# The first stage of an induced-attention and maxout kernel as one table of operations, with one group cut into a narrow and four shorter chunks

## The chip, the core and the metric

The kernel runs on one core of one Trainium2 chip. The metric is the device time of one execution in microseconds. The core has five engines that run their own instruction streams in order and wait for each other through semaphores: TensorE (PE, with PEld for its weight loads), VectorE (DVE), ScalarE (ACT), GpSimd (POOL), and SyncE (SP), which here issues nearly all DMA transfers.

## What is computed

The reference attends twice and then applies a maxout layer. Shapes: x is 4 x 12544 x 128, inducing is 32 x 128, w1, w2 and w3 are 128 x 768, w_out is 768 x 128.

```python
def mab(q, kv):
    s = scale * (q @ kv.transpose(0, 2, 1))
    s = s - s.max(-1, keepdims=True)
    a = np.exp(s)
    a /= a.sum(-1, keepdims=True) + 1e-09
    return a @ kv
h = mab(I, x)
return mab(x, h).astype(np.float32)
...
h = np.maximum(np.maximum(x @ w1, x @ w2), x @ w3)
return (h @ w_out).astype(np.float32)
```

In the first attention 32 inducing rows look at all 12544 tokens of a batch and give h, 32 x 128. In the second each token looks at the 32 rows of h. Its result goes through the maxout of three products and then through w_out.

## The kernel before

**Tiling.** A batch has 98 tiles of 128 tokens. They lie in seven groups: group 0 is short (2 tiles), groups 1 to 6 have 16 tiles each. Phase 1 is the first attention and works by group; it ends in hT, the transposed h divided by its sums. Phase 2 works by chunk: the short group is one chunk of 256 columns, and a full group gives four chunks of 512 columns. So a batch has 25 chunks and the kernel 100. Each chunk is six slots, one for each 128 of the 768 hidden columns.

**Algebra.** Since an output row of the second attention is probabilities times h, h is multiplied into the weights ahead of time (`first_products` for batch 0, `combine_products` later): wcat holds w1 - w2 and w3 - w2 in pairs and, in its last 128 columns, w2 times w_out (`prep_products`, kept by `keep_products`). The products of h with wcat are kept as a high and a low part in us. A slot is then: a matmul pu (L669), a relu by ACT (L684), a matmul pv (L675), a maximum by DVE (L702), a rounded copy hi by ACT (L691), the remainder lo by POOL (L699) or, for the slots listed in LOWVEC, by DVE (L705), and three matmuls into the accumulator (L727, L728, L729), six slots later (LAG). The first slot of a chunk adds one matmul with the last columns of us (L726).

**Weights.** They arrive as 64-bit numbers. `convert` makes 32-bit ones in steps: t, T, p, r and d on DVE, z on ACT, A (an addition) on POOL or, as a, on DVE, and S (subtraction of w2) on POOL. The digit in front is the matrix: 0 is w2, 1 is w_out, 2 is w1, 3 is w3. WORK lists which steps stand in which round of phase 1.

**Phase 1 of batch 0** is written out in `phase1_first`. For a group: load, 16 PE transposes (L272) with ACT copies (L274), products with the inducing rows (`attend_products`), maximum (`attend_max`), a column of it (`attend_column`), its spread over partitions by a matmul (`attend_spread`), the least value (`attend_least`), exponentials (`attend_weights`), a transpose (`attend_transpose`), sums on PE (`attend_sums`) and their copy (`attend_keep`). Then the groups are joined with weights (`combine_least` to `combine_states`). LOADS sets the order of the first transfers: short group, group 1 in four pieces, group 2, w2, group 3, w_out, groups 4 and 5, w1, group 6, w3. There are five buffers for full groups (XB).

**Filling.** Behind hT, the string ORDER interleaves the softmax of groups 0 (a) and 1 (b), the first products, dummy matmuls (`keep_busy`, d) and the first slots (s), until `main` runs the rest by a plan of slots. Phase 1 of batch b + 1 runs within phase 2 of batch b. `probs` brings the probabilities of a chunk into place: by PE transposes for the short group, by four DMAs on SP for the others.

All five engines keep the order in which the program writes their instructions (`manual_schedule`).

Of the kernel before, what the change touches and what calls it, by code (L numbers as in the profile page):

```python
# [8 lines left out]
F32 = mybir.dt.float32  # L9
# [16 lines left out]
def kernel(ctx, tc, x, xt, ind_t, w1, w2, w3, w_out, out):  # L26
    nc = tc.nc
# [23 lines left out]


    ORDER = "a a a a b a a b 0 c d m b a b a b a p d b 1 c s b b b s S m b q 2 c s 3 c s d s s d s"
# [70 lines left out]
    raws = []  # L124
    def first_loads():
        for what in LOADS:
            if what < NG:
                xg_next[(0, what)] = load_group(0, what, pieces=4 if what == 1 else 1)
            else:
                raws.append(load_raw(srcs[what - NG]))  # L130
# [79 lines left out]
    w2t = []  # L210

    def transpose_w2():
        for h in range(2):
            tpw = bank_v[h]
            for k in range(3):
                j = 3 * h + k
                nc.tensor.transpose(out=tpw[:, k * P : (k + 1) * P], in_=wf[:, 0, j * P : (j + 1) * P], identity=ident)
            w2h = hp.tile([P, 512], F32, name="w2h", tag="ru", bufs=3)
            nc.scalar.copy(out=w2h[:, : 3 * P], in_=tpw[:, : 3 * P])
            w2t.extend(w2h[:, k * P : (k + 1) * P] for k in range(3))  # L220

    def prep_products():

        wo = wf[:, 1, :].rearrange("p (j c) -> p j c", c=C)
        pw = bank_u[1]
        for j in range(NJ):
            nc.tensor.matmul(out=pw[:, :C], lhsT=w2t[j], rhs=wo[:, j, :], start=(j == 0), stop=(j == NJ - 1))

    def keep_products():
        nc.scalar.copy(out=wcat[:, 2 * DF :], in_=bank_u[1][:, :C])  # L230

    def prep_out():
        wo = wf[:, 1, :].rearrange("p (j c) -> p j c", c=C)
        nc.scalar.copy(out=wo_hi, in_=wo)
        nc.gpsimd.tensor_sub(out=wo_lo, in0=wo, in1=wo_hi.bitcast(F32))

# [3 lines left out]
    def start_batch(b):  # L240
        st = state[b] = {"xT": {}, "xg": {}, "a": {}, "s": {}}
# [25 lines left out]
    def transpose_x(b, gi, k):  # L267
        st = state[b]
        n = min(4, groups[gi]["nt"] - k)
        tps = (bank_u + bank_v)[k // 4]  # L270
        for i in range(n):
            nc.tensor.transpose(out=tps[:, i * P : (i + 1) * P], in_=st["xg"][gi][:, k + i, :], identity=ident)  # L272
        xv4 = st["xT"][gi].rearrange("p (q t l) -> p t q l", q=NQ, l=M)
        nc.scalar.copy(out=xv4[:, k : k + n, :, :], in_=tps[:, : n * P].rearrange("p (t q l) -> p t q l", q=NQ, l=M))  # L274
# [12 lines left out]
    def attend_max(b, gi):  # L287
# [5 lines left out]
        st["mq"] = mq  # L293

    def attend_column(b):
# [3 lines left out]
        nc.scalar.mul(out=md, in_=quad, mul=st["mq"])  # L299
        st["md"] = md  # L300

    def attend_spread(b, bank=None):
# [3 lines left out]
        nc.tensor.matmul(out=st["mp"][:, :NQ], lhsT=sel, rhs=st["md"], start=True, stop=True)  # L306
# [91 lines left out]
    def phase1_first():  # L398

        start_batch(0)  # L400
        nc.sync.dma_start(out=iT, in_=ind_t)
        nc.scalar.mul(out=iT, in_=iT, mul=scale)
        first_loads()
        def half(gi, k):
            if gi < NG:
                if k == 0:
                    start_group(0, gi)
                for i in (k, k + 4):
                    transpose_x(0, gi, i)

        start_group(0, 0)
        keep_busy(6, bank_o[1])
        transpose_x(0, 0, 0)
        keep_busy(2, bank_o[1])
        attend_products(0, 0, bank_a[0])
        attend_max(0, 0)
        attend_column(0)
        half(1, 0)
        attend_spread(0, bank_o[0])
        attend_least(0, 0)  # L420
        half(1, 8)
        work(WORK[0])
        st = state[0]
        for gi in range(NG - 1):
            last = gi == NG - 2
            attend_products(0, gi + 1, bank_a[(gi + 1) % 2])
            attend_weights(0, gi)
            half(gi + 2, 0)
            attend_max(0, gi + 1)
            attend_column(0)  # L430
            half(gi + 2, 8)
            if gi > 0:
                attend_sums(0, gi - 1, bank_o[1])
                attend_keep(0, gi - 1)
            attend_transpose(0, gi)
            if not last:
                work(WORK[gi + 1][0])
            attend_spread(0, bank_o[0])
            attend_least(0, gi + 1)
            if gi == 3:  # L440
                transpose_w2()
            if last:
                prep_products()
            else:
                work(WORK[gi + 1][1])
        combine_least(st)
        work(WORK[NG - 1])
        combine_weights(st)
        attend_weights(0, NG - 1)
        keep_products()  # L450
        attend_sums(0, NG - 2, bank_o[1])
# [536 lines left out]
```

## Time and profile before

| | us |
|---|---|
| median of three runs | 822.78 (822.32 to 823.0) |
| span of the profiled execution | 821.3 |
| hT written (end of L514) | 42.41 |
| first matmul of a 512-column chunk (L669) | 54.39 |
| first accumulation of group 2 of batch 0 (L726) | 93.99 |

The profile is of one execution. Its span runs from the first to the last instruction; the time of a run includes what lies around it. "L272" is line 272. In rows of an engine's order of time the first number is the start, the second the time covered, and brackets give the idle time in front and who ended it. Rows of groups give the count, the total busy time and the mean of one in ns.

### The profile page before, as it was taken

To read this page: it belongs to the slowest core of one execution; us is meant where nothing else is said; L and a number is where in the kernel's file an instruction comes from. 1 tells how busy PE (TensorE), PEld (TensorE's weight loads), DVE (VectorE), ACT (ScalarE), POOL (GpSimd) and SP (SyncE) were. 2 spreads that over 40 slices of the span, in tenths; PEclk is the share of its full clock that TensorE was granted. 3 is DMA by queue.
4 is the path that set the end of the run, shared out by engine and by line. 5 is a ranking of instruction groups with operands and counts; after the bars stand their busy time and mean duration, and the time that the engine had idled before them with its cause. 6 is when DMAs were issued, how large, how long until landed. Compare 5 with 4: busy or idle time off the path is not lost.

```text
span 821.3 us, 14725 instructions
## 1 busy us (share of the span) xinstructions
PE 809.0 (98%) x4604; PEld 634.0 (77%) x4604; DVE 627.4 (76%) x1090; ACT 743.5 (91%) x1558; POOL 650.1 (79%) x521
## 2 busy tenths in 40 slices
PE   7989999999999999999999999999999999999998
PEld 5757778778788787777778777877778788787886
DVE  4977778777787687787786877877778788778864
ACT  5779889898899898898999988989889899899996
POOL 1269779778799697787888977977879889888887
PEclk9999999999999999999999999999999999999999
DMA  8844534433443544344334352431223222222221
GB/s 325 310 137 151 188 88 161 161 120 107 136 139 121 154 154 162 84 162 159 110 106 142 116 205 83 159 119 58 63 80 89 71 78 77 65 81 76 63 78 52
DMA packets 44206, 102.51 MB, mean 125 GB/s; under 512 B 9568, under 2 KB 13536, under 8 KB 38880
## 3 DMA queue, kind: packets, MB, share of 16 engines
q1 hardware_dynamic: 43984, 101.44, 38.5%
q8 instruction: 37, 0.61, 0.3%
q14 instruction: 41, 0.34, 0.1%
q10 hardware_dynamic: 144, 0.13, 0.0%
HBM read 48.12 MB, written 25.69 MB: 90 GB/s over the span
## 4 chain that ended last, share of the span: by engine, by line
PE 95%; DMA 2%; DVE 1%; SPq 1%; ACT 1%; issue 0%; ACTq 0%; DVEq 0%
PE acc L727 17%; PE pv L675 16%; PE acc L728 16%; PE acc L729 16%; PE pu L669 16%; PE aux L585 3%; PE acc L726 3%; PE acc L346 3%; PE aux L282 2%; DMA xg<-in_x_dram 2%; PE acc L306 0%; PE pu L272 0%; SPq L100 0%; PE pv L272 0%; PE aux L551 0%; DMA pT<-pl 0%
## 5 line engine op out<-in xcount | busy, mean ns | idle before, releaser
L699 POOL TENSOR_TENSOR lo<-h,hi 128x512 fp32r<-128x512 f32 (+1 forms) x502 | 634.9, 1295 | 129.8 <-ACT hi L691 84.0
L702 DVE TENSOR_TENSOR h<-pv,ru 128x512 f32<-128x512 f32 (+1 forms) x600 | 404.2, 675 | 167.8 <-PE pv L675 81.2
L684 ACT ACTIVATE ru<-pu 128x512 f32<-128x512 f32 (+1 forms) x600 | 375.3, 626 | 52.6 <-PE pu L669 49.7
L691 ACT CAST hi<-h 128x512 fp32r<-128x512 f32 (+1 forms) x600 | 386.4, 644 | 0.4 <-DVE h L702 0.3
L727 PE MATMUL acc<-hi,wo_hi 128*128 128x512 f32 (+1 forms) x600 | 236.9, 395 | 0.0
L675 PE MATMUL pv<-pT,us 128*128 128x512 f32 (+1 forms) x600 | 232.1, 387 | 0.3 <-DVE h L702 0.3
L669 PE MATMUL pu<-pT,us 128*128 128x512 f32 (+1 forms) x600 | 231.5, 386 | 0.4 <-DMA pT<-pl 0.4
L728 PE MATMUL acc<-hi,wo_lo 128*128 128x512 f32 (+1 forms) x600 | 231.5, 386 | 0.0
L729 PE MATMUL acc<-lo,wo_hi 128*128 128x512 f32 (+1 forms) x600 | 231.2, 385 | 0.0
L727 PEld LDWEIGHTS acc<-hi,wo_hi 128*128 128x128 f32 x600 | 112.7, 188 | 30.0 <-issue 8.7
L675 PEld LDWEIGHTS pv<-pT,us 128*128 128x128 f32 x600 | 112.6, 188 | 24.2 <-DVE h L702 1.6
L669 PEld LDWEIGHTS pu<-pT,us 128*128 128x128 f32 x600 | 112.6, 188 | 23.9 <-DMA pT<-pl 0.6
L729 PEld LDWEIGHTS acc<-lo,wo_hi 128*128 128x128 f32 x600 | 112.7, 188 | 23.0
L728 PEld LDWEIGHTS acc<-hi,wo_lo 128*128 128x128 f32 x600 | 112.8, 188 | 21.1
L705 DVE TENSOR_TENSOR lo<-h,hi 128x512 fp32r<-128x512 f32 x98 | 71.3, 727 | 0.7 <-ACT hi L691 0.7
L744 ACT COPY o<-acc 128x512 f32<-128x512 f32 (+1 forms) x99 | 61.1, 617 | 0.0
L726 PE MATMUL acc<-pT,us 128*128 128x512 f32 (+1 forms) x100 | 38.7, 387 | 0.0
L346 PEld LDWEIGHTS acc<-xg,aT 128*32 128x32 f32 x768 | 21.1, 110 | 11.4 <-issue 6.8
L282 PE MATMUL aux<-xT,iT 128*32 128x512 f32 x192 | 25.3, 598 | 1.6 <-ACT xT L274 1.6
L346 PE MATMUL acc<-xg,aT 128*32 128x128 f32 x768 | 25.6, 274 | 0.0
L585 PE MATMUL aux<-xT,hT 128*32 128x512 f32 x192 | 25.1, 603 | 0.0
L192 POOL TENSOR_TENSOR rest<-rest,t 128x768 f32<-128x768 f32 x3 | 5.5, 1824 | 24.3 <-DVE rest L184 24.3
(119 smaller groups left out, 445.4 us busy)
## 6 DMA issues: line engine op xcount, KB each, us to landing
out_dram<-o SPq DMA_DIRECT2D x95, 256.0 KB, 2.0
xg<-in_x_dram SPq DMA_DIRECT2D x23, 1024.0 KB, 6.9
xT<-in_xt_dram SPq DMA_DIRECT2D x18, 1024.0 KB, 5.2
pT<-ph SPq DMA_DIRECT2D x192, 64.0 KB, 2.0
pT<-pl SPq DMA_DIRECT2D x192, 64.0 KB, 2.0
raw<-in_w_dram SPq DMA_DIRECT2D x3, 768.0 KB, 9.5
us<-uh SPq DMA_DIRECT2D x24, 52.0 KB, 1.9
us<-ul SPq DMA_DIRECT2D x24, 52.0 KB, 1.9
```

Of the source, the lines that this page charges most:

```text
L346: nc.tensor.matmul(out=hps[q * M : (q + 1) * M, :C], lhsT=aT[:, t * M : (t + 1) * M], rhs=xg[:, t, :], start=(t < NQ), stop=(t + NQ >= nt),)
L669: nc.tensor.matmul(out=pu[:, :w], lhsT=state[c.b]["us"][:, 2 * j * P : (2 * j + 1) * P], rhs=c.pT[:, :w], start=True, stop=True)
L675: nc.tensor.matmul(out=pv[:, : d.w], lhsT=state[d.b]["us"][:, (2 * j + 1) * P : (2 * j + 2) * P], rhs=d.pT[:, : d.w], start=True, stop=True,)
L684: nc.scalar.activation(out=ru[:, :w], in_=pu[:, :w], func=AF.Relu)
L691: nc.scalar.copy(out=hi[:, : c.w], in_=h[:, : c.w])
L699: nc.gpsimd.tensor_sub(**args)
L702: nc.vector.tensor_max(out=h[:, : d.w], in0=pv[:, : d.w], in1=relus.pop(s)[:, : d.w])
L705: nc.vector.tensor_sub(**low)
L726: nc.tensor.matmul(out=c.acc[:, :w], lhsT=us[:, 2 * DF :], rhs=c.pT[:, :w], start=True, stop=False)
L727: nc.tensor.matmul(out=c.acc[:, :w], lhsT=wo_hi[:, j, :], rhs=c.hh[j][:, :w], start=False, stop=False)
L728: nc.tensor.matmul(out=c.acc[:, :w], lhsT=wo_lo[:, j, :], rhs=c.hh[j][:, :w], start=False, stop=False)
L729: nc.tensor.matmul(out=c.acc[:, :w], lhsT=wo_hi[:, j, :], rhs=c.hl[j][:, :w], start=False, stop=(j == NJ - 1))
```

## The change

Batch 0's phase 1 and the filling behind it become one string of operations, FIRST, that is walked through once; each engine gets its part in that order. Capital letters are the steps of a group (T transposes, C their copies, P products, M maximum, D column, R spread, N least, E exponentials, X transpose, S sums, K their copy); digit and letter are the weight steps as before; c, l, i and hT join the groups; qS, qA and qB are the score products of the short group, the first four tiles of group 1 and its other twelve; s, a and b are the steps of their softmaxes; U, h, l, g and H are the first products, their high parts, low parts on DVE, copies and low parts on POOL; s with a digit is a slot and z a step of the second stage.

- The short group is last in phase 1 (TURN), and the loads are: group 1 in two pieces, groups 2 and 3, w2, group 4, w1, group 5, w3, group 6, the short group, w_out. The inducing rows are loaded from ACT's queue. XB is 6.
- Of w_out's work, d, the rounded copy, the remainder, and the product with w2 stand behind hT, as does half of w2's transposes. The addition for w3 is POOL's. The dummy matmuls are nine at the start and none behind hT.
- Group 1 of batch 0 is five chunks: one of 4 tiles over all quadrants (512 columns, probabilities by PE transposes, as for the short group) and four of 384 columns. Batch 0 has 26 chunks, the kernel 101. The lists LOWHEAD and LOWREST say which of their remainders DVE makes.
- The second stage starts four slots behind the first, not six, until slot 16.
- The score products of group 2 of batch 0 move from ORDER to the plan of the main loop.

```diff
-    XB = 5
+    XB = 6
-    LOADS = (0, 1, 2, 7, 3, 8, 4, 5, 9, 6, 10)
-    WORK = (
-        "",
-        ("0t 0T 0p 0z", "0r 0A"),
-        ("1t 1T 1p 1z", "1r 1A"),
-        ("0d 1d", "2t"),
-        ("2T 2p 2z", "2r 2A"),
-        ("3t 3T 3z", "3p 2d 2S"),
-        "3r",
-        "3a 3d 3S",
-    )
+    LOADS = (1, 2, 3, 7, 4, 9, 5, 10, 6, 0, 8)
+    TURN = (1, 2, 3, 4, 5, 6, 0)
+    HEAD = 4
+    LOWHEAD = (1, 4)
+    LOWREST = (0, 17, 19, 21, 23)
+    FIRST = (
+        "B9 B4 T11 T10 T12 C10 C11 T13 C12 C13 P1 T20 C20 M1 T21 D1 T22 T23 R1 N1 C21 C22 C23 E1 T30 T31 T32 "
+        "P2 C30 X1 T33 C32 0t C31 C33 M2 0T S1 D2 R2 P3 T42 0p N2 0r 0z T43 M3 K1 E2 D3 C43 X2 0A T40 R3 S2 "
+        "2t N3 T41 C40 C42 2T T50 2p T53 E3 0d T52 C41 C50 C53 X3 T51 C52 C51 2r P4 2A 2z M4 3t P5 M5 K2 D4 "
+        "R4 N4 T62 T61 T60 T63 3z D5 E4 3T 2d C61 C60 C63 3p R5 S3 C62 X4 N5 1t 2S T00 P6 3r K3 E5 C00 1z M6 "
+        "S4 P0 X5 M0 D6 K4 R6 N6 D0 E6 W1 1T R0 S5 n2 N0 X6 3A cl E0 1p K5 S6 cw X0 lw 1r cm 3d lt iv K6 S0 "
+        "1A cg123456 K0 w1 cg0 hT W0 qS 1d qA 3S aT sT qB w0 am Oh sm ax ae sx bT se U1 sr U0 ar si h1 ai sp "
+        "g1 ap su sh au bm sl U2 ah bx js h0 h2 ks al l0 Ol Gp H1 be g2 Gk s0 br bi bp ja ka s1 bu U3 H2 n3 "
+        "s2 4h s3 4l bt s4 bh s5 bl y2 z0 s6 y3 z1 s7 z2 s8 z3 z4 s9 s10 z5 s11 z6 s12 z7 "
     )
-    ORDER = "a a a a b a a b 0 c d m b a b a b a p d b 1 c s b b b s S m b q 2 c s 3 c s d s s d s"
...
-    def prep_out():
+    def prep_high():
+        nc.scalar.copy(out=wo_hi, in_=wf[:, 1, :].rearrange("p (j c) -> p j c", c=C))
+
+    def prep_low():
         wo = wf[:, 1, :].rearrange("p (j c) -> p j c", c=C)
-        nc.scalar.copy(out=wo_hi, in_=wo)
         nc.gpsimd.tensor_sub(out=wo_lo, in0=wo, in1=wo_hi.bitcast(F32))
...
-        nc.sync.dma_start(out=iT, in_=ind_t)
+        nc.scalar.dma_start(out=iT, in_=ind_t)
...
-    def scores_products(b, gi, bank):
+    def scores_products(b, gi, bank, first=0, last=None):
...
+                out=bank[q * M : (q + 1) * M, :n],
+                lhsT=st["hT"][:, :M],
+                rhs=xT[:, q * w + first * M : q * w + last * M],
...
     class Chunk:
-        def __init__(self, n, b, gi, q):
-            self.n, self.b, self.gi, self.q = n, b, gi, q
-            self.w = GT * M if q is not None else groups[gi]["nt"] * P
+        def __init__(self, n, b, gi, q, first=0, last=None):
+            self.n, self.b, self.gi, self.q, self.first = n, b, gi, q, first
+            self.last = last or groups[gi]["nt"]
+            self.w = (self.last - first) * (P if q is None else M)
...
-            if self.q is None or (self.gi == 1 and self.q == k == 0):
-                return False
+            if self.q is None:
+                return self.last == HEAD and k in LOWHEAD
+            if self.first == HEAD:
+                return NJ * self.q + k in LOWREST
...
+            parts_ = [(None, 0, None)]
+            if groups[gi]["nt"] == GT:
+                parts_ = [(q, 0, None) for q in range(NQ)]
+                if b == 0 and gi == 1:
+                    parts_ = [(None, 0, HEAD)] + [(q, HEAD, None) for q in range(NQ)]
...
-                elif b > 0 or g > 1:
+                else:
                     first.append((scores_products, b, g + 1, bank_a[0]))
...
-            if s >= LAG:
-                c, j = slots[s - LAG]
-                stage2(c, j)
-                if j == NJ - 1:
-                    over = c
+            if done[0] <= s - (LAG if s >= begins[0] + 4 else LAG - 2):
+                over = second()
```

More of the change, by code (lines that the diff above doesn't have):

```diff
@@ L265, in load_channels, with transpose_x, keep_x @@
         state[b]["xg"][gi] = xg_next.pop((b, gi))
[L267 to L274, printed above, removed]
+    def transpose_x(gi, i):
+        st = state[0]
+        if gi not in st["xT"]:
+            start_group(0, gi)
+        tps = (bank_u + bank_v)[i]
+        for k in range(min(4, groups[gi]["nt"])):
+            nc.tensor.transpose(out=tps[:, k * P : (k + 1) * P], in_=st["xg"][gi][:, 4 * i + k, :], identity=ident)
+    def keep_x(gi, i):
+        n = min(4, groups[gi]["nt"])
+        tps = (bank_u + bank_v)[i]
+        xv4 = state[0]["xT"][gi].rearrange("p (q t l) -> p t q l", q=NQ, l=M)
+        nc.scalar.copy(
+            out=xv4[:, 4 * i : 4 * i + n, :, :], in_=tps[:, : n * P].rearrange("p (t q l) -> p t q l", q=NQ, l=M)
+        )
     def attend_products(b, gi, bank):
@@ L529, in first_products @@
         st["up"][which] = up, st["us"][:, cs]
+    half = slice(2 * M, P)
     def first_high(st, which):
@@ L731, in finish @@
     def finish(c):
-        at = groups[c.gi]["at"] + (c.q or 0) * c.w
+        g = groups[c.gi]
+        at = g["at"] + (c.q or 0) * g["nt"] * M + c.first * M
         o = op.tile([P, 512], F32, name="o", tag="o", bufs=3)
+        if c.q is None and c.last < g["nt"]:
+            nc.scalar.copy(
+                out=o.rearrange("p (q t l) -> p t q l", q=NQ, l=M), in_=c.acc.rearrange("p (t q l) -> p t q l", q=NQ, l=M)
+            )
+            nc.sync.dma_start(
+                out=out[c.b, :, at : at + g["nt"] * P].rearrange("p (q n) -> p q n", q=NQ)[:, :, : c.w // NQ],
+                in_=o.rearrange("p (q n) -> p q n", q=NQ),
+            )
+            return
         if c.n == len(chunks) - 1:
@@ L756 @@
         for gi in range(NG):
-            full = groups[gi]["nt"] == GT
-            for q in range(NQ) if full else [None]:
-                chunks.append(Chunk(len(chunks), b, gi, q))
-    nch = len(chunks) // B
+            parts_ = [(None, 0, None)]
[3 more added lines that the diff above has]
+                    parts_ = [(None, 0, HEAD)] + [(q, HEAD, None) for q in range(NQ)]
+            for part in parts_:
+                chunks.append(Chunk(len(chunks), b, gi, *part))
     LAG = 6
@@ L765 @@
     plan = [[] for _ in range(len(slots) + LAG)]
-    per_batch = nch * NJ
-    short = NJ if groups[0]["nt"] < GT else 0
+    begins = [min(c.n for c in chunks if c.b == b and c.q is not None) * NJ for b in range(B)]
     WIN = NQ * NJ
@@ L801 @@
     for b in range(B):
-        base = b * per_batch + short
+        base = begins[b]
         n = b + 1
@@ L870, with second, main @@
             burst(s0 + 15, *second)
-    def main():
-        over = None
-        for s in range(len(slots) + LAG + 1):
+    done = [0]
+    def second():
+        c, j = slots[done[0]]
+        done[0] += 1
+        stage2(c, j)
+        return c if j == NJ - 1 else None
+    def main(start, over):
+        for s in range(start, len(slots) + LAG + 1):
             if s >= LAG:
@@ new lines @@
+        for step in FIRST.split():
+            kind, rest = step[0], step[1:]
+            if step in names:
+                names[step]()
+            elif kind in steps and not rest.isdigit():
+                next(steps[kind])
+            elif kind == "c":
+                combine_groups(st, [int(g) for g in rest[1:]], bank_u[0])
+            elif kind.isdigit():
+                convert(int(kind), rest)
+            elif kind == "s":
+                advance()
+            elif kind == "z":
+                if over:
+                    finish(over)
+                over = second()
+            elif kind == "f":
+                finish(over)
+                over = None
+            elif kind == "y":
+                probs(tails[rest])
+            else:
+                one[kind](*[int(v) for v in rest])
@@ L934 @@
+        for gen in steps.values():
+            assert next(gen, None) is None
+        main(pipe["next"], over)
 _GT = 16
```

304 lines of the change are left out of this document (139 added, 165 removed).

## The prediction

> **What bounds the kernel now.** I began with the page's busy shares. Then I cut the span into stages, and inside the first of them I read each engine's instructions in order of time.
>
> ```profile
> span 821.3 us, 14725 instructions
> PE 809.0 (98%) x4604; PEld 634.0 (77%) x4604; DVE 627.4 (76%) x1090; ACT 743.5 (91%) x1558; POOL 650.1 (79%) x521
> 10.00:20.00 10.00, 8.06 (x64) 4.67 (x64) 6.79 (x11) 7.89 (x18) 2.32 (x2) 1.00 1.03 410
> 13.54:42.41 28.87, 25.68 (x347) 18.50 (x346) 26.05 (x45) 21.34 (x52) 9.64 (x7) 1.00 0.85 319
> 42.41:54.39 11.98, 10.14 (x62) 5.50 (x62) 9.67 (x24) 8.03 (x21) 6.46 (x7) 1.00 0.37 114
> 54.39:60.92 6.53, 6.53 (x43) 5.37 (x44) 4.80 (x9) 5.94 (x13) 5.32 (x6) 1.00 0.64 185
> 60.92:93.99 33.07, 33.07 (x190) 25.25 (x188) 25.36 (x45) 30.37 (x67) 27.43 (x23) 1.00 0.53 173
> 93.99:800.00 706.01, 706.01 (x3822) 557.17 (x3821) 548.44 (x945) 657.30 (x1368) 585.25 (x465) 1.00 0.36 113
> ```
>
> The columns of the stages are length, then busy time of PE, PEld, DVE, ACT and POOL, granted clock, DMA share and GB/s. From 60.92 us on PE has no gap. What the change does after group 1 of batch 0 therefore costs or brings nothing, unless it alters PE's own work; PE's 706.01 of 706.01 us is the cover. The time is decided by when PE gets there. My marker is the first accumulation of group 2 of batch 0 (L726, at 93.99 below): after it both kernels have the same PE work left. So the forecast is where that marker lands.
>
> ```profile
> 55.31 0.28 PE L726 MATMUL acc<-pT,us 128*128 128x256 f32 x1
> 55.42 0.27 PE L727 MATMUL acc<-hi,wo_hi 128*128 128x256 f32 x1
> 93.99 0.39 PE L726 MATMUL acc<-pT,us 128*128 128x512 f32 x1
> 94.21 0.39 PE L727 MATMUL acc<-hi,wo_hi 128*128 128x512 f32 x1
> ```
>
> Durations overlap; the pitch of starts is what a matmul costs: 0.22 to 0.23 us with 512 columns (I use 0.2265), 0.11 to 0.12 with 256 (0.115). This is almost proportional, so 384 columns should pitch at 0.171. Before the marker lie two stages, split by h (the tile hT, which ends at 42.41).
>
> **Part 1, up to h: VectorE's list.** DVE is busy 26.05 of the 28.87 us between its first weight step and hT.
>
> ```profile
> 0.75 0.39 SPq L401 DMA_DIRECT2D iT<-in_ind_t_dram  x1
> 1.19 0.42 SPq L100 DMA_DIRECT2D xgs<-in_x_dram  x1
> 13.54 0.56 DVE L171 TENSOR_SCALAR t<-raw 128x768 uint32<-128x768 uint32 x1 [0.97 <-DMA raw<-in_w_dram]
> 14.14 0.96 DVE L175 SCALAR_TENSOR_TENSOR t<-raw,t 128x768 uint32<-128x768 uint32 x1
> 15.13 0.56 DVE L180 TENSOR_SCALAR pw<-t 128x768 uint32<-128x768 uint32 x1
> 15.61 0.15 DVE L312 TENSOR_REDUCE mneg<-acc 128x1 f32<-128x4 f32 x1
> 15.72 0.96 DVE L184 SCALAR_TENSOR_TENSOR rest<-raw,pw 128x768 f32<-128x768 uint32 x1
> 16.60 0.68 DVE L292 TENSOR_REDUCE mq<-aux 128x1 f32<-128x512 f32 x1
> 17.20 0.70 DVE L336 STREAM_TRANSPOSE aT<-a 128x512 f32<-128x512 f32 x1
> ...
> 37.37 0.38 DVE L477 TENSOR_TENSOR sw<-sel,w 128x224 f32<-128x224 f32 x1
> ...
> 38.53 0.95 DVE L192 TENSOR_TENSOR rest<-rest,t 128x768 f32<-128x768 f32 x1
> 39.51 0.96 DVE L196 SCALAR_TENSOR_TENSOR dst<-size,rest 128x768 f32<-128x768 f32 x1
> 41.66 0.35 DVE L509 RECIPROCAL rec<-rec 128x32 f32<-128x32 f32 x1
> 42.12 0.29 DVE L514 TENSOR_TENSOR hT<-pu,rec 128x128 f32<-128x128 f32 x1
> ```
>
> Where the list starts: w2's raw weights land at 13.54 (DVE waited 0.97 us for them). The new load order puts groups 1, 2 and 3 ahead of w2 and takes the short group out, so 0.9 MB more stands in front: 2.2 us at 410 GB/s. The first big load leaves SP where iT now leaves, 0.9 us sooner than in before, since iT moves to ACT's queue and the short group back; its pieces are also larger. I credit 1.0 us (bounds 0 and 1.5). So w2 lands at about 14.7, between 14.2 and 15.7.
>
> What is in the list: after this point the table has for DVE four of t, T, p, r (by the starts above 0.60, 0.98, 0.50, 0.90: 11.9), three d (0.95 each: 2.85), the maxima and transposes of groups 2 to 6 (0.60 and 0.62 each: 6.1) and of group 0 (an estimate of 0.4), six least-values (0.9), and the joining steps up to hT (the rows of sw, rec and hT, 1.0, and four of about 0.1 each: 1.45). Sum 23.6. The addition of row 38.53 (0.95) goes to POOL. The d of w_out moves behind hT. Both leave the list.
>
> What it waits for: once for group 2's products, which now stand behind three transposes of group 3 on PE (0.25), and small hand-overs, for which I take 0.8 of the 2.8 us that DVE idles in this stage now (bounds 0 and 2.8). And one thing that the new order creates:
>
> ```profile
> L196 DVE SCALAR_TENSOR_TENSOR wf<-size,rest x2: 945/1298/1652, 22.8 to 24.4; 128x768 f32<-128x768 f32 x2
> 21.81 1.83 POOL L192 TENSOR_TENSOR rest<-rest,t 128x768 f32<-128x768 f32 x1 [2.66 <-DVE rest L184]
> ```
>
> A d that starts while POOL is in an addition takes 1.65 us, not 0.95: it ends about 0.8 us after POOL's end at 23.64. In the table the steps "1r cm 3d" run directly after each other, and POOL begins w_out's addition when 1r ends. So 3d waits for most of its 1.83 us; hT needs the group sums on PE anyway, so I take 1.15 us of this (bounds 0 and 1.4). Sum: 14.7 + 23.6 + 0.25 + 0.8 + 1.15 = 40.5, say **hT at 40.6, 1.8 us sooner**. PE and ACT do not set it: each loses w_out's work here, and their busy times (25.68 and 21.34) stand under DVE's.
>
> **Part 2, from h to the marker.**
>
> ```profile
> 42.85 0.27 DVE L598 STREAM_TRANSPOSE aux<-aux 128x64 f32<-128x64 f32 x1 [0.44 <-PE aux L585]
> 50.42 1.22 SPq L654 DMA_DIRECT2D pT<-ph  x2
> 54.39 0.50 PE L669 MATMUL pu<-pT,us 128*128 128x512 f32 x1 [0.38 <-DMA pT<-pl]
> 54.98 0.60 ACT L684 ACTIVATE ru<-pu 128x512 f32<-128x512 f32 x1 [0.84 <-PE pu L669]
> 55.48 0.40 ACT L691 CAST hi<-h 128x256 fp32r<-128x256 f32 x1
> 55.77 0.61 ACT L684 ACTIVATE ru<-pu 128x512 f32<-128x512 f32 x1
> 56.26 0.41 ACT L691 CAST hi<-h 128x256 fp32r<-128x256 f32 x1
> L217 PE MATMUL pv<-ident,wf 128*128 128x128 f32 x6 | 0.9, 282 | 0.0
> L227 PE MATMUL pu<-wf,w2h 128*128 128x128 f32 x12 | 1.6, 282 | 0.0
> L219 ACT COPY w2h<-pv 128x384 f32<-128x384 f32 x2 | 0.9, 537 | 0.0
> L234 ACT CAST wo_hi<-wf 128x768 fp32r<-128x768 f32 x1 | 0.8, 835 | 0.0
> L396 PE MATMUL pu<-ident 128*128 128x128 f32 x16 | 2.6, 287 | 0.6 <-ACT pT L651 0.5
> ```
>
> Now hT to the marker takes 51.58 us. PE's work in it is 10.14 less 2.6 of dummy matmuls (L396), then, for the six short slots after 54.39, twelve 512-column and eighteen 256-column matmuls and a few others (5.25 of 6.53), then 33.07: 45.8. Slack is 5.8.
>
> Moved in: half of w2's transposes (0.45), the six products with w_out (1.6), four transposes for the 4-tile chunk (0.75, by the mean of the 128-column rows). The six extra slots bring 31 matmuls but no columns: at pitches 0.2265 and 0.171 that is 0.1. Together 2.9. The dummies go; they cost nothing, as they stood in slack.
>
> The slack that stays: the table puts w_out's d first behind hT on DVE, and POOL's subtraction 3S, released by 3d, is then running, so by the row above it ends some 1.75 us after hT, at 42.35. Behind it on DVE wait both score transposes, which now start at 42.85; this gains only 0.5 us there. From there ACT is the dense engine: w_out's cast 0.8, exponentials and probability copies 2.0, six evictions of first products at 0.5, w2's product 0.2, twelve evictions of the short chunk at 0.29 (the pitch of the 256-column rows; 512 pitch at 0.49) less one, 3.3: 9.3, with hand-overs 9.8. So the 4-tile chunk's first relu comes at about 52.2, against 54.98, without the DMA wait in row 54.39, as its probabilities come from PE transposes. Between hT (40.6) and there PE has 10.0 us of work in 11.6: slack 1.6. Over the next six slots ACT again asks 0.8 to 1.0 a slot, and I leave 0.8. Together 2.4, against 5.8. Behind the 4-tile chunk the 384-column chunks get their probabilities by DMA, issued when the larger softmax ends, about 52.3; in before it took 4 us from issue (row 50.42) to use (row 54.39), and the head's six slots cover some 6.
>
> Sum: 45.8 + 2.9 + 2.4 = 51.1 after hT: the marker at 91.7 against 93.99. **The span falls by 2.3 to 819.0.** The runs' median 822.78 stands 1.5 above the profiled span, and I keep that: **820.5**.
>
> One rule speaks against taking the dummies out. The granted clock is 1.00 in every stage above, also with PE busy 8.06 of 10 us. The Trainium skill, "TensorE: Matmul & The Clock Gate", in its part on the HAM clock gate, says that the clock halves after an idle window of some 3.4 us. The trace has no gap so long with which to test it.
>
> **Rivals.**
> - *The hand-overs stay* (chance 0.22). DVE waits its 2.8 us and the lock in full; hT comes at 42.6 or later, and only the shorter filling gains. Against before: 0 to 1, so about 822.3. For it: the same chain of maximum, column, spread and least runs once per group in both. Against it: the table puts a weight step between its parts.
> - *ACT becomes the bound; slower* (0.12). ACT's busy time from hT to the marker is 8.03 + 5.94 + 30.37 = 44.3 of 51.6. Added: the cast, one copy of w2 and the product (1.5), the evictions (at an interpolated 0.39 for 384 columns, 48 of them and 12 of 512 against 48 of 512: 1.1), copies for the split softmax (1.0): 47.9. If the 7.3 us that it now idles stay, the marker is at 40.6 + 55.2 = 95.8 and the time 824.6. It decides from 5.5 us of idle on. Against it: ACT's idle is mostly waiting in the filling, which the table is dense in.
> - *The filling is tighter* (0.10): no lock on 3d and 1d, w2 at 14.2, hT at 39.2 and 50.3 to 51.1 behind it; the marker at 89.5 to 90.3, so 818.3 to 819.1. With no hand-overs either it is 817.5.
> - *The clock drops behind hT* (0.02), where the dummies stood: at half pace PE's 10.0 us there take 20 in place of 11.6, so about 829.
>
> **How the numbers follow.** The forecast has 0.54, with a range of its own of 819 to 821.8 from w2's landing and the hand-overs. A measurement of this kernel can tell about 0.2% (1.65 us) from no change: faster is below 821.1, slower above 824.4. Faster: 0.46 of the forecast, the tighter filling's 0.10 and 0.01 of the first rival, 0.57. Slower: most of the ACT case and the clock, 0.12. Same: 0.31. The range from 816.8 to 823.8 leaves out most of the ACT case, the clock and the end of the tighter filling, under 0.2.
>
> **What would show it.** Right: w2's first step on DVE near 14.7; hT ending between 39.5 and 41.5; 3d and the d behind hT over 1.3 us long; the first 512-column relu near 52; no dummies and under 3 us of PE gaps behind hT; the marker near 91.7; the same 706 us behind it. Wrong: a marker shift other than the shift of the span, which would mean that the change works in the later part; a PE that waits for ACT or POOL in the 384-column chunks; a granted clock under 1.00; hT no sooner than 42.

## The result and the profile after

The changed kernel takes 827.84 us (median of 5, 826.8 to 828.18) against 822.78 (822.32 to 823.0): a ratio of 1.0057, with a 95% interval of 1.0042 to 1.0072. It is slower by 5.06 us, outside the range of the prediction, and on the side that was given a chance of 0.12. The description of the change has one slip: the table begins with thirteen dummy matmuls ("B9 B4"), not nine.

Of the page after, the first line; then a cut into the stages that the prediction used (hT ends at 42.31, the short chunk's first accumulation starts at 53.80, that of the 4-tile chunk at 59.46, the marker is at 96.37). Columns as before: length, busy time of PE, PEld, DVE, ACT, POOL, granted clock, DMA share, GB/s.

```profile
span 825.8 us, 15091 instructions
```

```profile
13.54:42.31 28.77, 24.54 (x342) 16.90 (x339) 27.19 (x45) 20.87 (x52) 10.36 (x7) 1.00 0.52 197
42.31:53.80 11.49, 8.65 (x61) 5.41 (x61) 11.15 (x30) 8.12 (x23) 6.34 (x6) 1.00 0.79 327
53.80:59.46 5.66, 5.54 (x32) 4.58 (x32) 4.60 (x9) 5.36 (x14) 4.75 (x6) 1.00 0.19 47
59.46:96.37 36.91, 36.87 (x241) 30.39 (x239) 29.38 (x59) 33.03 (x83) 27.13 (x26) 1.00 0.56 180
96.37:800.00 703.63, 702.43 (x3803) 553.56 (x3802) 550.51 (x944) 653.06 (x1361) 579.10 (x458) 1.00 0.36 113
```

```profile
96.37 0.40 PE L694 MATMUL acc<-pT,us 128*128 128x512 f32 x1
```

The marker moved from 93.99 to 96.37, by +2.38; the span grew by 4.5. So about half of the loss arises ahead of the marker and half behind it, where PE, busy 706.01 of 706.01 us before, now has 1.2 us of gaps in 703.63. Before hT, DVE is busy 27.19 of 28.77 us (26.05 of 28.87 before), although steps were taken off it.

**Ahead of hT.** The changed kernel's DVE in order of time, rows of weight steps, and POOL's rows beside the long ones:

```profile
15.36 0.52 DVE L171 TENSOR_SCALAR t<-raw 128x768 uint32<-128x768 uint32 x1
...
25.77 1.79 DVE L171 TENSOR_SCALAR t<-raw 128x768 uint32<-128x768 uint32 x1
...
31.04 1.51 DVE L171 TENSOR_SCALAR t<-raw 128x768 uint32<-128x768 uint32 x1
...
38.86 2.56 DVE L196 SCALAR_TENSOR_TENSOR dst<-size,rest 128x768 f32<-128x768 f32 x1
...
42.02 0.29 DVE L462 TENSOR_TENSOR hT<-pu,rec 128x128 f32<-128x128 f32 x1
42.46 1.74 DVE L196 SCALAR_TENSOR_TENSOR wf<-size,rest 128x768 f32<-128x768 f32 x1
```

```profile
25.33 1.82 POOL L192 TENSOR_TENSOR rest<-rest,t 128x768 f32<-128x768 f32 x1 [4.49 <-DVE rest L184]
30.05 2.07 POOL L200 TENSOR_TENSOR wcat<-dst,wf 128x768 f32<-128x768 f32 x1 [2.90 <-DVE dst L196]
...
38.72 1.89 POOL L192 TENSOR_TENSOR rest<-rest,t 128x768 f32<-128x768 f32 x1 [3.35 <-DVE rest L184]
...
41.57 1.81 POOL L200 TENSOR_TENSOR wcat<-dst,wf 128x768 f32<-128x768 f32 x1 [0.70 <-DVE rec L456]
```

Read the two together. Every stretched row overlaps a POOL row and ends 0.4 us (t) to 0.8 us (d) after it: the t at 25.77 ends at 27.56, POOL's addition at 27.15. So do a t at 20.08 (1.19) and a T at 34.90 (1.28), not shown. The t that overlaps none takes 0.52. The same line in the kernel before (ns: least, median, most) shows no such stretch; its longest, 694, is the one that overlaps the end of a POOL addition:

```profile
L171 DVE TENSOR_SCALAR t<-raw x4: 560/578/694, 13.5 to 31.5; 128x768 uint32<-128x768 uint32 x4
```

The Trainium skill, "SBUF — State Buffer", section "Who interferes with whom", has tensor_scalar in its two-port modes, and operations with two inputs in SBUF, use ports that DVE shares with GpSimd; whoever comes first holds them for a whole instruction, and the other blocks. The rows agree: 1.79 against 0.52 us. Below this is called the lock.

**Behind the marker.** PE's first accumulations of the short chunk of batch 1 and of the chunk behind it, before and after, then DVE's and POOL's rows after:

```profile
250.07 0.28 PE L726 MATMUL acc<-pT,us 128*128 128x256 f32 x1
256.55 0.40 PE L726 MATMUL acc<-pT,us 128*128 128x512 f32 x1
```

```profile
252.46 0.28 PE L694 MATMUL acc<-pT,us 128*128 128x256 f32 x1
258.39 0.51 PE L640 MATMUL pv<-pT,us 128*128 128x512 f32 x1 [0.47 <-DVE h L667]
259.94 0.40 PE L694 MATMUL acc<-pT,us 128*128 128x512 f32 x1
```

```profile
256.14 1.59 DVE L670 TENSOR_TENSOR lo<-h,hi 128x512 fp32r<-128x512 f32 x1 [0.94 <-PE acc L697]
257.66 0.68 DVE L667 TENSOR_TENSOR h<-pv,ru 128x512 f32<-128x512 f32 x1
```

```profile
255.89 1.29 POOL L664 TENSOR_TENSOR lo<-h,hi 128x512 fp32r<-128x512 f32 x1 [1.75 <-ACT hi L656]
```

The distance is 6.48 us before and 7.48 after. DVE makes a remainder (L670) that waits 0.94 for PE to free its buffer and takes 1.59, and the next maximum stands behind it. The median of this line is 0.68; here POOL's own remainder, from 255.89 to 257.18, lies in its way, so the lock seems to have a part in this too. Behind the short chunk of batch 2 the distance grows alike, from 6.47 to 7.48 us; behind that of batch 3 it is 7.23 in both kernels. The diff ahead of the prediction shows why: the old condition `self.q is None or (self.gi == 1 and self.q == k == 0)` kept the first slot of group 1 of every batch off DVE; its second half went. The list of changes doesn't name it, and the prediction gives it no price.

### The profile page after: what moved, and what is told of

It reads as the page before. It is cut to its first block, busy times and chain, and to the rows that moved or that the text cites. A ratio compares the mean times of both kernels' runs of the same rounds, so it can differ in the third digit from the quotient of the medians.

```text
span 825.8 us, 15091 instructions
## 1 busy us (share of the span) xinstructions
PE 811.1 (98%) x4641; PEld 638.7 (77%) x4641; DVE 638.6 (77%) x1110; ACT 744.8 (90%) x1574; POOL 648.1 (78%) x521
## 4 chain that ended last, share of the span: by engine, by line
PE 95%; DVE 3%; ACT 1%; issue 0%; POOL 0%; ACTq 0%; DVEq 0%; POOLq 0%
PE acc L695 17%; PE pv L640 16%; PE acc L696 16%; PE acc L697 16%; PE pu L634 16%; PE aux L538 3%; PE acc L694 3%; PE aux L289 2%; PE acc L355 2%; PE pu L405 1%; PE pu L273 1%; PE acc L315 0%; PE pv L273 0%; DVE h L667 0%; DVE wf L196 0%
## 5 line engine op out<-in xcount | busy, mean ns | idle before, releaser
L664 POOL TENSOR_TENSOR lo<-h,hi 128x512 fp32r<-128x512 f32 (+2 forms) x501 | 631.0, 1290 | 137.2 <-ACT hi L656 94.1
L667 DVE TENSOR_TENSOR h<-pv,ru 128x512 f32<-128x512 f32 (+2 forms) x606 | 405.1, 670 | 159.6 <-PE pv L640 99.0
L649 ACT ACTIVATE ru<-pu 128x512 f32<-128x512 f32 (+2 forms) x606 | 375.2, 619 | 53.5 <-PE pu L634 50.4
L656 ACT CAST hi<-h 128x512 fp32r<-128x512 f32 (+2 forms) x606 | 386.9, 638 | 1.8 <-DVE h L667 1.5
L695 PE MATMUL acc<-hi,wo_hi 128*128 128x512 f32 (+2 forms) x606 | 238.0, 393 | 0.0
L640 PE MATMUL pv<-pT,us 128*128 128x512 f32 (+2 forms) x606 | 233.9, 386 | 1.8 <-DVE h L667 1.4
L634 PE MATMUL pu<-pT,us 128*128 128x512 f32 (+2 forms) x606 | 233.3, 385 | 0.2 <-ACT ru L649 0.2
L696 PE MATMUL acc<-hi,wo_lo 128*128 128x512 f32 (+2 forms) x606 | 232.7, 384 | 0.0
L697 PE MATMUL acc<-lo,wo_hi 128*128 128x512 f32 (+2 forms) x606 | 232.5, 384 | 0.0
L670 DVE TENSOR_TENSOR lo<-h,hi 128x512 fp32r<-128x512 f32 (+1 forms) x105 | 77.8, 741 | 4.2 <-PE acc L697 2.7
```

The lines of the kernel that those rows point to most:

```text
L634: nc.tensor.matmul(out=pu[:, :w], lhsT=state[c.b]["us"][:, 2 * j * P : (2 * j + 1) * P], rhs=c.pT[:, :w], start=True, stop=True)
L640: nc.tensor.matmul(out=pv[:, : d.w], lhsT=state[d.b]["us"][:, (2 * j + 1) * P : (2 * j + 2) * P], rhs=d.pT[:, : d.w], start=True, stop=True,)
L649: nc.scalar.activation(out=ru[:, :w], in_=pu[:, :w], func=AF.Relu)
L656: nc.scalar.copy(out=hi[:, : c.w], in_=h[:, : c.w])
L664: nc.gpsimd.tensor_sub(**args)
L667: nc.vector.tensor_max(out=h[:, : d.w], in0=pv[:, : d.w], in1=relus.pop(s)[:, : d.w])
```

## The experiments

Theory A: two faults, the dropped exclusion (behind the marker) and POOL in the way of DVE (ahead of hT), hide a table that works as forecast. Rivals: the small additions of the softmax, the second stage's early start, the clock, the split. Runs are compared by medians; the number of executions and the range stand in brackets. The kernel before, run beside them, had medians of 822.59 to 822.86.

**The first slot.** e1_slot0 puts the exclusion back into the changed kernel; e2_before_slot0 takes it out of the kernel before.

```diff
+            if self.gi == 1 and self.q == k == 0:
+                return False
             return NJ * self.q + k in (LOWVEC if self.b + 1 < B else LOWLAST)
```

> The changed kernel, with one condition of before put back: the remainder of slot 0 of group 1 in batches 1 to 3 is POOL's again and not DVE's. The marker (first accumulation of group 2 of batch 0) stays at 96.4 us. Theory A (DVE is late at that slot behind the short chunk of batches 1 and 2, 1.0 us each, the two steps by which the kernels drift apart from +2.4 to +4.4 us): the drift after the marker goes, the time falls by 2.0 us to about 825.8. Rival (more load buffers or the third softmax buffer shift something there): the drift stays, the time stays within 0.5 us of 827.8.

825.79 us (11, 824.64 to 826.24), ratio 1.0028 (1.0017 to 1.0039): 2.05 less, as theory A asked. The marker is hardly moved (96.25), and the distance is 6.48 again:

```profile
252.35 0.28 PE L696 MATMUL acc<-pT,us 128*128 128x256 f32 x1
...
258.83 0.40 PE L696 MATMUL acc<-pT,us 128*128 128x512 f32 x1
```

> The kernel before, with that condition taken out: slot 0 of group 1 is DVE's in all four batches. Theory A: PE waits for DVE behind the short chunks of batches 1 and 2, 1.0 us each, and perhaps in batch 0: 2 to 3 us more than 822.8, so 824.8 to 825.8. Rival: within 0.5 us of 822.8.

826.55 us (8, 826.01 to 829.46), ratio 1.0042 (1.0025 to 1.0059): the old kernel loses 3.9, more than expected. Here the edit acts in batch 0 too, where the changed kernel has lists of its own (LOWHEAD, LOWREST); in its profiled execution (828.29) the distance behind batch 0's short chunk is 7.64 us (55.00 to 62.63), in the kernel before 5.61 (55.31 to 60.92). So the surplus shows there.

**POOL beside DVE.** e4_poolshort leaves POOL's two conversion steps all their instructions and waits, but only 16 of 768 columns for A and 4 of each 128 for S, so most of w1 - w2, w3 - w2 and the corrections is not computed; wcat is filled with zeros first.

```diff
-            (nc.gpsimd if step == "A" else nc.vector).tensor_add(out=c["rest"], in0=c["rest"], in1=c["t"].bitcast(F32))
+            nc.gpsimd.tensor_add(out=c["rest"][:, :16], in0=c["rest"][:, :16], in1=c["t"].bitcast(F32)[:, :16])
```

> The changed kernel, with POOL's weight additions and subtractions in phase 1 cut to a few columns (wcat is set to zero at the start; the conversion is left incomplete). Theory B: DVE's steps beside them fall to their lengths alone (t from 1.19, 1.79 and 1.51 to 0.56 us; 3d from 2.56 to 0.95; the d of w_out from 1.74 to 0.95), hT comes 3.5 to 5.5 us sooner, near 37 to 39 in place of 42.3, and the time falls by 3 to 5 us. Rival C (the load order or the chain through PE and ACT sets hT): DVE's steps shorten, but hT stays within 1.5 us of 42.3 and DVE waits instead.

823.88 us (12, 822.97 to 824.52), ratio 1.001 (1.0 to 1.0019): 3.96 less than the changed kernel. hT ends at 39.70, not at the 37 to 39 that theory B asked. DVE's rows in order of time:

```profile
16.81 0.52 DVE L172 TENSOR_SCALAR t<-raw 128x768 uint32<-128x768 uint32 x1
...
37.46 0.97 DVE L197 SCALAR_TENSOR_TENSOR dst<-size,rest 128x768 f32<-128x768 f32 x1
...
39.41 0.29 DVE L463 TENSOR_TENSOR hT<-pu,rec 128x128 f32<-128x128 f32 x1 [0.49 <-PE pu L437]
39.62 0.95 DVE L197 SCALAR_TENSOR_TENSOR wf<-size,rest 128x768 f32<-128x768 f32 x1
```

From the first t to the end of hT it is 22.89 us, against 26.95: the lock costs 4.06 there, and 0.79 more in the d behind hT. The first t itself comes 1.45 later: POOL fills wcat before it makes the identity matrix that PE's first matmuls read, and PE starts at 2.79 in place of 1.37. So this run understates the lock.

**e12_both: both remedies,** the exclusion back in and POOL's two steps short. The addition keeps 16 of 768 columns, a forty-eighth, not an eighth as the expectation has it.

> The kernel of e4_poolshort (POOL's two conversion steps on an eighth and a thirty-second of their columns: the same instructions, orders and waits, almost none of POOL's time, output not the reference's) with the exclusion of e1_slot0 put back. If the two losses (2.05 us behind the short chunk, 4 us by POOL beside DVE in the first phase) are separate, they add: 823.88 - 2.05 = 821.8, within 0.5, which is below the kernel before; if they overlap (the short chunk's gap is partly the same slack), 822.4 to 823.9.

821.52 us (11, 820.83 to 822.25), ratio 0.9982 (0.9973 to 0.9991). The losses add; without them the table is 1.2 us faster than the kernel before, though it leaves out most of POOL's part of the conversion.

**e3_eps: the additions of 1e-9 on ACT.** DVE's first additions behind hT, a pair in the changed kernel and one in the kernel before:

```profile
45.97 1.13 DVE L567 TENSOR_SCALAR rs<-rs 128x2 f32<-128x2 f32 x2
```

```profile
44.57 0.17 DVE L611 TENSOR_SCALAR rs<-rs 128x2 f32<-128x2 f32 x1
```

```diff
-        if b == 0 and gi < 2:
+        if False:
```

> The changed kernel, with the three small additions of 1e-9 in the filling of batch 0 on ACT and not on DVE. Theory B (a tensor_scalar of DVE waits for the end of a POOL operation that reads SBUF): the 1.13 us of two additions beside POOL's remainder of w_out and the 1.27 us of the third, against 0.17 each alone, go; ACT's take 0.35 each. The first relu of the 4-tile chunk, at 55.36, comes 0.5 to 1.5 us sooner and the time falls by as much. Rival (ACT sets the filling): ACT's three operations make it 0 to 1 us longer.

828.09 us (6, 826.55 to 828.59), ratio 1.0056 (1.004 to 1.0073): no gain. DVE now waits for ACT instead, and in the profiled execution the clock was halved from 36 to 46 us, so the run doesn't isolate them:

```profile
47.87 0.18 DVE L571 RECIPROCAL rs<-rs 128x4 f32<-128x4 f32 x1 [1.16 <-ACT rs L569]
```

```profile
36.00:46.00 10.00, 9.57 (x81) 0.51 0.54 198
```

(Columns of this and the next windows: length, PE busy, granted clock, DMA share, GB/s.)

**Reordering against the lock.** e5_nolock and e9_order are e1_slot0 with another table: 3t ahead of 2r, w_out's t and T ahead of 2d, 3r, 3A and 2S, and w_out's p, r and A behind hT, five buffers; e9 also has dummies ("B4", "B2", "B3" and the like), and 1p and 1r directly behind hT. The core of e9:

```diff
-        ... X3 T51 C52 C51 2r P4 2A 2z M4 3t P5 ... S3 C62 X4 N5 1t 2S T00 P6 3r K3 E5 ... 3A cl E0 1p ... 1r cm 3d lt iv K6 S0 1A cg123456 ...
+        ... X3 T51 C52 C51 3t 2r P4 2A 2z M4 P5 ... N5 S3 C62 X4 1t T00 P6 E5 1T 2d 3r 3A 2S K3 ... cm 3d lt iv K6 S0 B3 cg123456 K0 w1 cg0 hT W0 B3 qS 1p qA 3S 1r ...
```

> The first experiment's kernel (slot 0 of group 1 on POOL again) with a reordered table: DVE's weight steps stand where no weight operation of POOL runs (3t before 2r; w_out's t and T, then 2d and 3r before POOL's 3A and 2S, with maxima and transposes beside those), w_out's p, r and POOL's addition for it move behind hT, and with them its d, cast and product; XB is 5. Theory B (waits of DVE for POOL, 4 us up to hT): hT comes at 38.5 to 39.5 in place of 42, the time falls by 2 to 3.5 us against 825.8, to about 822.3 to 823.8. Theory C (the filling behind hT is full by itself on ACT and DVE): hT comes as early, but the first relu of the 4-tile chunk comes no more than 1 us sooner, and the time stays at 825 or above.

831.82 us (5, 829.65 to 833.23), ratio 1.0101 (1.0079 to 1.0123). A miss: PE waits for operations that my order put too late, and the clock falls with it.

```profile
PE pu L634 <- POOL us L495: 2.5, 1, 2.5
```

```profile
36.00:42.00 6.00, 5.62 (x75) 0.52 0.02 4
...
54.00:60.00 6.00, 3.47 (x16) 0.50 0.19 68
```

> The first experiment's kernel with a second reordering against the waits of DVE for POOL, and dummies in the gaps: 3t before 2r; w_out's t and T, then 2d and 3r before POOL's 3A and 2S, beside which stand maxima and transposes; w_out's p and r directly behind hT, its addition on POOL after 3S, its d and cast five steps later than now; XB is 5. Theory B: hT at 39.5 to 40.5 in place of 42, the clock at 1.00, and the time falls by 1.5 to 3 us against 825.8, to 822.8 to 824.3. Theory C (the filling is full by itself): hT as early, but the marker no more than 0.5 us sooner than 94.

824.43 us (12, 824.06 to 825.53), ratio 1.0012 (0.9999 to 1.0025): 1.36 less than e1_slot0, short of the 1.5 to 3 that theory B asked; hT ends at 40.80 and the marker is at 95.01. An order can avoid part of the lock: the t's at 23.44 and 28.92 take 0.52 each. The sums that hT waits for then stand behind the dummies:

```profile
40.51 0.29 DVE L462 TENSOR_TENSOR hT<-pu,rec 128x128 f32<-128x128 f32 x1 [2.25 <-PE pu L436]
```

**The clock, the early second stage.** e8_busy is e1_slot0 with 22 dummies in PE's waits between group 0's products and the short chunk ("B4", "B2", "B3", "B3", "B5 B5"); e7_pause lets the second stage start later.

```diff
-            if done[0] <= s - (LAG if s >= begins[0] + 4 else LAG - 2):
+            if done[0] <= s - (LAG if s >= begins[0] + 15 else LAG - 1 if s >= begins[0] + 2 else LAG - 2):
```

> The first experiment's kernel with 22 dummy matmuls put back into PE's gaps near and behind hT (four before the group spread, two, three and three around the join, ten before the short group's probability transposes). In earlier profiles of variants without dummies the granted clock fell to 0.5 for some 4 us near there, in others it stayed at 1.00. Theory E (part of the changed kernel's loss is this clock, in some of the executions): the clock stays 1.00 and the median falls by 0.5 to 1.5 us below 825.8. Rival (the drop falls into slack when it comes): the time stays within 0.4 us of 825.8, or rises by what dummies in front of real matmuls cost, up to 0.5.

825.28 us (11, 824.69 to 826.15), ratio 1.0023 (1.0011 to 1.0034): 0.5 less, the lower end of theory E, with a mean clock of 0.999 or 1.000 in every execution. So the clock has a small part. Of the changed kernel's own five executions, three had a mean clock of 0.993 to 0.996 and took 827.84 to 828.18 us; the other two, at 0.999 and 1.000, took 826.8 and 827.77, still 4 us or more behind the kernel before. The clock is not what makes the change slow.

> The first experiment's kernel with the second stage falling back from four to six slots behind in two steps, at slots 14 and 27, where other matmuls stand, and not in two slots running from 16 on. Theory D (with two slots without second stage PE waits for ACT and DVE, some 1.3 us near 67 to 69 us): those gaps go and the time falls by 0.5 to 1.3 us, to 824.5 to 825.3. Rival: the gaps only move, the time stays within 0.4 us of 825.8.

825.33 us (11, 824.44 to 825.92), ratio 1.003 (1.0019 to 1.004): 0.46 less, between the two theories. The first accumulations of the 4-tile chunk and of the first and last 384-column chunk start at 58.36, 66.58 and 86.08 us (in e1_slot0 at 59.30, 68.36 and 87.16; the profiled execution of e7_pause was ahead from its first t on). The first distance falls from 9.06 to 8.22 us, the second grows from 18.80 to 19.50: most of the gain is given back.

**The split.** e6_nosplit has group 1 whole, as before; e10_nosplit_busy adds the dummies.

```diff
-                if b == 0 and gi == 1:
-                    parts_ = [(None, 0, HEAD)] + [(q, HEAD, None) for q in range(NQ)]
```

> The first experiment's kernel with group 1 of batch 0 left whole (four chunks of 512 columns, probabilities by DMA; the table ends at slot 6). If the split earns what I put on it (the first 512-column chunk without the DMA wait, against six slots of fixed costs): 1 to 2 us longer, 826.8 to 827.8. If the split costs more than it brings (fixed cost of 31 matmuls and 18 evictions, PE waits in the 384-column slots): 1 to 2 us shorter, about 824.

831.67 us (4, 831.15 to 832.1), ratio 1.01 (1.008 to 1.012). PE waits 4.6 us for the probabilities' DMA, which the split avoids, and then works at half clock:

```profile
PE pu L625 <- DMA pT<-pl: 4.6, 1, 4.6
```

```profile
60.00:64.00 4.00, 4.00 (x16) 0.50 0.59 128
```

> The kernel with group 1 left whole (831.7 us, clock 0.5 for parts of the filling) with dummies in PE's gaps, 18 of them before the first 512-column slot that waits for its probabilities. Theory E: the clock stays 1.00 and 2 to 4 us of the 5.9 that it lost against the split one come back, to about 828 to 829.5; what is left is the wait for the DMA of the probabilities, the price of not splitting. Rival (the clock matters little): 831 or more.

830.8 us (6, 829.28 to 833.67), ratio 1.009 (1.0067 to 1.0112). By the median only 0.87 of the 5.9 comes back, as the mean clock was still 0.995 in three executions. The three with a mean clock of 1.000 took 829.28 to 829.55, those of e8_busy 824.69 to 825.28: the split earns 4.0 to 4.9 us in this table.

**The start.** The chain of waits of the changed kernel, in its first 14 us, begins so (start, length, what):

```profile
1.37 5.71 PE pu L405 x26
7.08 0.89 PE pu L273 x8
7.99 2.06 ACT xT L279 x4
```

The first transposes stand behind the thirteen dummies, which leave 26 records, and these run slowly: in the changed kernel most start 0.21 us apart, in e11_order2 the last twelve 0.11. Line L405 in the changed kernel and in e11_order2 (below), records of 128 columns (ns: least, median, most):

```profile
L405 PE MATMUL pu<-ident x26: 275/421/579, 1.4 to 6.8; 128*128 128x128 f32 x26
```

```profile
L405 PE MATMUL pu<-ident x54: 273/275/579, 1.4 to 45.5; 128*128 128x128 f32 x54
```

Ten kernels here begin with the same dummies at 1.37 us (the changed one, e1, e3 and e5 to e11). In their profiled executions the 26 records took 4.58 to 5.92 us, and the first t came 9.65 to 9.86 us later than that length, at 14.23 to 15.77. So one execution's first t can differ from another's by 1.5 us with no edit at the start.

e13_start, e14_best and e15_free leave out "B4" at the start: of e1_slot0, of e11_order2, and of e12_both, where the fill is also DVE's. e11_order2 is e9_order without two "B3" and with the edit of e7_pause.

> The kernel of e9_order without the three dummy blocks before the group sums and the three before the score product qS (hT there waited 2.25 us for the group sums), and with the later second products of e7_pause (worth 0.46 us there). If the dummies lie in the path of hT, hT comes 0.5 to 0.9 us sooner than the 40.80 of e9_order and with the pause the time is 823.0 to 823.7; if PE's own chain to the marker has no slack left, the time stays at 824.2 to 824.6; if the missing dummies let the clock drop, it is above 825.

824.0 us (11, 823.09 to 824.57), ratio 1.0011 (1.0002 to 1.002): 0.43 less, between the first two cases; hT ends 0.82 sooner, as the first asked.

> e1_slot0 with the first four-dummy block left out: nine dummies (18 records) before the first transposes, not thirteen (26). Theory S: the chain of waits starts with the dummies (5.71 us, 12.7% of the chain up to 45 us), and VectorE's list starts behind that chain, not behind w2's landing. The first records take 421 ns, twice the later 273, so the clock rises only during them; with eight records less at 0.11 to 0.22 us the first transposes start at 5.0 to 5.5 (now 6.8), run partly at the slow pace, and the first weight step starts 0.7 to 1.3 us sooner (now 15.2); hT follows by as much, and the time is 824.6 to 825.1 against 825.79. Rival L: the data of group 1's second piece or w2's landing set it (w2 landed 10.2 us or more behind its issue at 2.6); then the first weight step moves less than 0.4 us and the time less than 0.3.

825.85 us (12, 825.18 to 826.99), ratio 1.003 (1.0018 to 1.0041): no gain, as rival L asked, but not shown to be for its reason. The first t starts at 14.67, 0.55 sooner than in e1_slot0 and inside the spread above; the first eight transpose records, now run at the slow pace, take 1.88 us in place of 1.04. hT ends 0.51 sooner. The profiled execution, the slowest of the twelve, then runs at a lower clock for a while (the rows are of the start, of the wait for the probabilities behind hT, and of the window behind that). But the six executions with a mean clock of 1.000, 825.18 to 825.66 us, show no gain either, so where the 0.51 goes isn't settled.

```profile
5.37 1.88 PE L273 MATMUL pu<-ident,xg 128*128 128x128 f32 x8
...
47.78 0.37 PE L602 MATMUL pu<-ident_r,pn 128*128 128x128 f32 x2 [2.11 <-DVE pn L582]
```

```profile
48.00:54.00 6.00, 5.80 (x32) 0.72 0.48 197
```

> The best computing kernel so far, e11_order2 (824.0), with the same four-dummy block left out. Theory S: 0.5 to 1.1 us less, 822.9 to 823.5, not measurably different from the kernel before (822.7). Rival L: 823.7 to 824.3. If the clock then drops later because PE started colder, above 824.5.

823.14 us (12, 822.45 to 823.94), ratio 0.9992 (0.9979 to 1.0004): 0.86 less than e11_order2, as theory S asked. The profiled executions don't show it coming from the start: the first t is at 14.70 (14.34 in e11_order2), the end of hT at 40.36 (39.98). e14_best is the fastest that computes everything, and not told apart from the kernel before.

> e12_both (821.52) without two delays of the start: the fill of wcat is VectorE's, so that POOL makes the identity 1.4 us sooner (in e12_both PE started at 2.78, elsewhere at 1.37), and the four-dummy block is left out. POOL's two conversion steps stay shortened (output not the reference's). Theory S: the start of the chain sets hT one for one, so 1.4 to 2.3 us less: 819.2 to 820.1, close to the 820.5 that was predicted for a table without these losses. Rival L: the loads set the start, 820.9 to 821.6.

820.17 us (6, 820.07 to 820.26), ratio 0.9955 (0.9938 to 0.9972): 1.35 less than e12_both, a little under theory S's 1.4. It has two edits in one: PE starts 1.41 us sooner again, at 1.37, which alone is enough for the 1.35; what the four dummies bring is not told apart. Its first t, hT and marker:

```profile
14.20 0.52 DVE L172 TENSOR_SCALAR t<-raw 128x768 uint32<-128x768 uint32 x1
...
37.48 0.29 DVE L463 TENSOR_TENSOR hT<-pu,rec 128x128 f32<-128x128 f32 x1 [0.53 <-PE pu L437]
```

```profile
90.82 0.40 PE L697 MATMUL acc<-pT,us 128*128 128x512 f32 x1
```

## Why the prediction was wrong

The 827.84 us break down, by medians of runs, into the first slot (2.05), POOL beside DVE (3.96) and the 1.35 of e15_free. The last is no third fault of the table: that edit took back the delay that e4_poolshort's own fill had brought, and with it four dummies. Taken off, the three leave 820.5; e15_free measured 820.17. The prediction was 820.5, with 1.15 us of POOL beside DVE in it. That the table without these losses lands so near is in part luck: in e15_free hT came 2.8 us sooner than forecast, and the way from hT to the marker was 2.0 us longer.

- **"What the change does after group 1 of batch 0 therefore costs or brings nothing" failed.** PE's full 706 us were taken as cover for every later edit, with "unless it alters PE's own work" as the one exception. A step on DVE between PE's two products alters when PE may go on: 1.0 us each at the short chunks of batches 1 and 2. Shown by e1_slot0 and the distances 6.48 and 7.48. This is the step that missed the half of the loss behind the marker.
- **The lock was mis-sized.** The step took 1.15 us for 3d alone. It measured 4.06 up to hT, and it goes on behind hT (below). 3d took 2.56, 1.6 over its 0.95, as it must wait a whole POOL addition that starts just ahead of it; the rest are t's and a T, for which I used the starts of the kernel before. There the t's met almost no POOL operation; the new order puts them beside POOL's additions and subtraction. A duration from a row holds only for what ran beside that row.
- **Where the list starts.** I had 14.7, from w2's landing; it was 15.36, and DVE had just waited 1.35 us for ACT in the chain of group 1, not for the DMA. That chain starts behind the dummies, which the prediction gave no place. Between executions that start alike the first t lies anywhere from 14.23 to 15.77, so 14.7 was near for another reason than the one given.
- **The list itself was too long.** 23.6 of steps, 0.25 and 0.8 of waits were 24.65 without the lock; 22.89 in e4_poolshort. Together: hT was to be at 40.6 and came at 42.31.
- **hT to the marker was to take 51.1 and took 54.06.** Up to the first relu of the 4-tile chunk (55.36) it was 13.05 us, not 11.6; from there 41.01, not 39.5. In e15_free, without the lock on the conversion, the two are 12.02 (relu at 49.79) and 41.03. So some 1.0 us is the lock again, and 1.5 arises behind the relu, where that lock plays no part. By busy time the undersized term there is PE's work: 48.7 was to be and 51.06 was busy; of slack, 2.4 and 3.00. But busy time covers short waits: PE's matmuls at 67.49, 67.87, 68.22 and 68.50 start 0.28 to 0.38 us apart with no gap between them, where the pitch is 0.17. Up to 1.3 us is that six short slots were put at 5.25 of 6.53 us because that was their pitch; how the rest divides into work and waits stays open. In e15_free hT to the marker is still 53.05 (37.77 to 90.82), so this error and the one of the list cancel in part.
- **Right in kind:** the d behind hT ends 1.89 us after it (I had 1.75) and holds the score transposes behind it. 384 columns pitch at 0.17 to 0.18 us, near the interpolated 0.171; so in the changed kernel's order of time:

```profile
68.85 0.34 PE L696 MATMUL acc<-hi,wo_lo 128*128 128x384 f32 x1
69.03 0.34 PE L697 MATMUL acc<-lo,wo_hi 128*128 128x384 f32 x1
```

- **Of the rivals** none happened as told. ACT is busy 33.03 of the 36.91 us from the 4-tile chunk's first accumulation to the marker, and PE 36.87; short waits of PE hide in that, as above. The marker came at 96.37, near the ACT rival's 95.8, for other reasons. The hand-overs were not the matter, since DVE is busy 27.19 of 28.77 us; of that rival only the lock came. The clock was 1.00 in the profile of the changed kernel; it fell in other executions and variants. That hT came no sooner than 42, and that the marker moved by 2.38 but the span by 4.5, were among the signs that the prediction named for being wrong.

## What to carry to other kernels

Read every condition that a diff drops, and ask which engine's work it moves, even where the bound engine has no gap: a full engine covers only what stands in slack on the others. Before taking a VectorE duration from an old order, look at what GpSimd did in that moment, and list for the new order which pairs will overlap; a t of 0.52 us became 1.79 here. A big rearrangement is best judged by building the version without each suspected fault: such edits turned a loss of 5.06 us into a gain of 2.7, in a version that leaves most of POOL's part of the conversion out. Such a version must not bring a delay of its own, as the fill of wcat did here. And before an edit at the start is credited with a row of one profile, look at how far that row moves between executions: 1.5 us here. An order with that gain that computes everything was not found: e14_best ends level with the kernel before.

## What was not expected of the hardware

- **The start runs at half pace while the clock row says 1.00.** The first dummies' records start 0.21 us apart and take 421 ns, against 0.11 us and 275 ns later; the windows of the profile have a granted clock of 1.00 there. The 26 records took 4.58 to 5.92 us in ten kernels that are the same up to there, and the first t moved with them. The Trainium skill, "TensorE: Matmul & The Clock Gate", "Part 1: The HAM clock gate (the "warmup" mystery)", has the first 3.4 us or so of matmuls run at half clock, and the number of slow ones vary between runs. The rows agree that it varies; slow records lasted 2.9 us in e11_order2 and 5.9 in e5_nolock.
- **The clock falls after short waits.** In e13_start it was 0.72 in 48 to 54 us, where PE's wait shown above was 2.11 us. In e3_eps it was 0.51 in 36 to 46 us, and from 20 us up to there no wait of PE was over 1.2 us; the changed kernel's profile has the same waits there at a clock of 1.00. In the same part the page has the drop come after an idle window of some 3.4 us; no single wait in these two is so long, while e6_nosplit's 4.6 us, with half clock behind it, fits. What sets the drop isn't settled; with dummies no execution of e8_busy had a mean clock under 0.999, but three of e10_nosplit_busy had.
- **Tiny DVE operations seem to block too:** a pair of tensor_scalars on 128x2 numbers took 1.13 us beside POOL's subtraction (45.19 to 46.99), and one on 128x12, at 50.49, took 1.27 beside another (50.44 to 51.72). One on 128x2 took 0.17 in the kernel before, with POOL idle. This is read from the overlap; e3_eps doesn't isolate it.
